# Second layer of a spectral mixture-of-experts kernel: a unit's products in two pairs of runs instead of four

## The chip, the cores and the metric

One core of a Trainium2 chip runs the whole program. The metric is device time in microseconds: the median of the runs of one kernel. Below, PE is TensorE, DVE is VectorE, ACT is ScalarE, POOL is GpSimd and SP is the engine that issues most transfers.

## The reference

Three stages follow each other, all in float32. The change touches the last alone.

```python
def _moe2_ref(x, w_in, w_out):
    h = np.maximum(x @ w_in, 0.0)          # x: 24576 x 256, w_in: 256 x 2048
    return (h * h @ w_out)                 # w_out: 2048 x 256

def reference(**kwargs):
    attn_out = _attn_ref(...)              # filter by FFT over 3072 positions, 8 x 3072 x 256
    x = attn_out.reshape(B * S, D)
    x = _moe_ref(x=x, ...)                 # each token through one of 8 experts (256 -> 1024 -> 256)
    return _moe2_ref(x=x, ...)             # every token through a dense layer with squared ReLU
```

## The kernel before

The filter, the routing and the first (expert) layer come first; the second layer runs when they are done, from about 1775 us to the end. A float32 operand is held as two parts, a high part and the rest (`bh` and `bl` for x, `wsh` and `wsl` for w_in, `hh` and `hl` for the squared hidden values, `woh` and `wol` for w_out), and a product is made of three matmuls: high x high, high x rest, rest x high. Every matmul of this layer has a 128x128 stationary operand, which a weight load brings (LDWEIGHTS, PEld in the rows), and 256 moving columns.

The layer works on 48 tiles of 512 tokens (`NTILE2`), each in 8 units of 256 hidden values (`NU`): 384 units. A unit has two halves.

`up2` forms x @ w_in for a unit. By a scheme of Strassen's kind (seven block products in place of eight) it makes products with indices 0 to 6, three matmuls each, 21 in all. Three PSUM banks take them: V (`psH`, two buffers, tile name `ph`), G (`psX`, one buffer, tile name `px`) and P (`psH2`, one buffer, tile name `ph` too). V and G are added onto in stages: V holds product 0, then 0+4, then 0+4+5, then all with 2, and between two stages a copy or an addition reads it: ACT's copies `s1` (after 0), `u2` (after 4) and the last into `C[:, 2]`; DVE's addition into `C[:, 3]` (after 5). G holds product 3, which ACT copies to `p5`, then 3+6, which DVE adds into `C[:, 1]`. P holds product 1, which DVE adds into `C[:, 0]`. The next stage of a bank may start only when the reader of the stage before has ended. Below, V0, G3, P1, V4, G6, V5, V2 are the bank and the index of a product (a bank's name and a first index), and C0, C1, C3 the three additions. At the end DVE makes `q`, the squared ReLU of all four blocks of C.

`split_h` splits `q` for the second matrix: `hh` is a copy to the high part on ACT, `hl` the rest on DVE (q minus hh). `down2` multiplies them with w_out, 24 matmuls, and adds onto the tile's two banks `py` over its 8 units; at a tile's last unit ACT copies these (`ou`) and POOL sends the rows out.

All three are generators, and the loop in `steps_m` fixes by hand the order in which they issue: in turn n it advances `up2` of unit n, `split_h` of unit n-1 and `down2` of unit n-2. Each engine runs its instructions in that order. So TensorE's row in a turn is V0 G3, 3 of `down2`, P1 V4, 6, G6 V5, 9, V2, 6: four pairs of an `up2` run and a `down2` run. Once in a tile `split_t` prepares the next tile's operand in four steps at the ends of four turns: copies on ACT and subtractions on DVE (`tc` among them).

Of the kernel before, what the change touches and what calls it, by code (L numbers as in the profile page):

```python
# [17 lines left out]
ALU = mybir.AluOpType  # L18
# [84 lines left out]
def spectral_moe_kernel(ctx: ExitStack, tc: tile.TileContext, x, filt_r, filt_i, w_gate, w_og, w1, w2,  # L103
                        w_in, w_out, c_ma, c_mi, c_mb, c_mb2, c_sg, c_cum, out):
    nc = tc.nc
# [608 lines left out]
    def py_tiles(t):  # L714
        return [pl["psY2" if t % 2 and "psY2" in pl else "psY"].tile([128, TT], F32, name=f"py{h}") for h in range(2)]
# [82 lines left out]
    def up(t, f):  # L798
        xh, xl = X[t]
        w = width[t]  # L800
        h1, l1 = (a[:, 0] for a in W[t, f // 2])
        f2 = f % 2
        ps = ph_tile()[:, 0:w]
        n = 0
        for c in range(2):
            for a, b in ((h1, xh), (h1, xl), (l1, xh)):
                nc.tensor.matmul(ps, a[:, c, f2 * 128:(f2 + 1) * 128], b[:, c, 0:w], start=n == 0, stop=n == 5)  # L807
                n += 1
        hh = pl["hp"].tile([128, TT], F32R, name="hh")[:, 0:w]
        hl = pl["hp"].tile([128, TT], F32R, name="hl")[:, 0:w]  # L810
        nc.scalar.activation(hh, ps, AF.Relu)  # L811
        tick[:] = [hh[0:1, 0:1].bitcast(F32)]
        nc.vector.scalar_tensor_tensor(hl, ps, 0.0, hh.bitcast(F32), op0=ALU.max, op1=ALU.subtract)  # L813
        H[t, f] = hh, hl
# [77 lines left out]
    def up2(t, u):  # L892

        bh, bl, _ = X2[t]
        wsh, wsl = w2nd[0:2]

        def prod(ps, a, b, start):
            for n, (x, y) in enumerate(((wsh, bh), (wsh, bl), (wsl, bh))):
                nc.tensor.matmul(ps, x[:, u, a], y[:, b], start=start and n == 0, stop=n == 2, skip_group_check=True)  # L899

        bank = lambda name: pl[name].tile([128, TT], F32, name="px" if name == "psX" else "ph")[:, 0:256]
        V, G, P = bank("psH"), bank("psX"), bank("psH2")
        s1, p5, u2 = (pl["sp"].tile([128, 256], F32, name=n) for n in ("s1", "p5", "u2"))
        C = pl["cp"].tile([128, 4, 256], F32, name="C")
        prod(V, 0, 0, True)
        nc.scalar.copy(s1, V)
        prod(G, 3, 3, True)
        nc.scalar.copy(p5, G)
        yield
        prod(P, 1, 1, True)  # L910
        nc.vector.tensor_tensor(C[:, 0], P, s1, ALU.add)
        prod(V, 4, 4, False)
        nc.scalar.copy(u2, V)  # L913
        yield
        prod(G, 6, 2, False)
        prod(V, 5, 5, False)
        nc.vector.tensor_tensor(C[:, 3], V, p5, ALU.add)  # L917
        nc.vector.tensor_tensor(C[:, 1], G, u2, ALU.add)
        yield
        prod(V, 2, 6, False)  # L920
        nc.scalar.copy(C[:, 2], V)  # L921
        q = pl["cp"].tile([128, 4, 256], F32, name="q")
        nc.vector.scalar_tensor_tensor(q, C, 0.0, C, op0=ALU.max, op1=ALU.mult)  # L923
        H2[t, u] = q
        yield

    def split_h(t, u):
        q = H2[t, u]
        hh, hl = (pl["h2p"].tile([128, 4, 256], F32R, name=n) for n in ("hh2", "hl2"))
        nc.scalar.copy(hh, q)  # L930
        yield
        nc.vector.tensor_tensor(hl, q, hh.bitcast(F32), ALU.subtract)  # L932
        H2[t, u] = hh, hl
        yield

    def down2(t, u):

        hh, hl = H2[t, u]
        woh, wol = w2nd[2:4]
        if u == 0:  # L940
            Z[t] = [p.rearrange("p (c d) -> p c d", c=2) for p in py_tiles(t)]
        for m in range(24):
            k, i, c, n = m // 12, m // 6 % 2, m // 3 % 2, m % 3
            x, w = ((hh, woh), (hl, woh), (hh, wol))[n]
            nc.tensor.matmul(Z[t][k][:, c, :], x[:, 2 * i + k, c * 128:(c + 1) * 128], w[:, 2 * u + i, :],  # L945
                             start=u == 0 and m in (0, 12), stop=u == NU - 1 and m in (11, 23), skip_group_check=True)
            if u == NU - 1 and m in (11, 23):
                if k == 0:
                    Z[t].append(pl["oup"].tile([128, 4, D], F32, name="ou"))
                ou = Z[t][2]  # L950
                nc.scalar.copy(ou[:, 2 * k:2 * k + 2, :], Z[t][k])  # L951
                io = X2[t][2]
                for c in range(2 * k, 2 * k + 2):
                    nc.gpsimd.indirect_dma_start(out=outv[4 * t + c], out_offset=bass.IndirectOffsetOnAxis(ap=io[:, c:c + 1], axis=0),  # L954
                                                 in_=ou[:, c, :], in_offset=None)
            if m in (2, 8, 17):
                yield
        del H2[t, u]
        if u == NU - 1:
            del X2[t], Z[t]  # L960
        yield
# [3 lines left out]
    units2 = [(t, u) for t in range(NTILE2) for u in range(NU)]  # L965
# [3 lines left out]
    def step_1(t, f):  # L969

        last = t + 1 == KP
        if f == 5 and t + 2 == KP:
            start_t(KP)
        if f == 1 and t + 1 >= KP:
            for n in (t + 2, t + 3) if last else (t + 3,):
                if n < NMAIN:
                    start_t(n)
        if f == 1 and last:
            gather(KP)
        if f == 3 and t + 2 < NMAIN and t + 2 != KP:  # L980
            gather(t + 2)
        if f % 2 == 1:

            g = NQ * t + f // 2 + 2
            if NQ * KP <= g < NQ * NMAIN:
                split_w(*divmod(g, NQ))
            if NQ * KP <= g + 2 < NQ * NMAIN:
                load_w(*divmod(g + 2, NQ))
        if t + 1 < NMAIN:
            at = (4, 5, 7) if last else (2, 4, 6)  # L990
            if f == at[0]:
                scale_x(t + 1)
            if f == at[0] + 1:
                put_ids(t + 1)
            if f in at[1:]:
                turn_x(t + 1, at.index(f) - 1)
        elif f == 1:
            load_t(0)
            load_t(1)
        if f not in (1, 5) and dec and next(dec[0], 0) == 0:  # L1000
            dec.clear()
            dcs.close()
            pl["bp0"] = ctx.enter_context(tc.tile_pool(name="bp0", bufs=1))
            pl["bp0"].tile([128, 16], F32, name="pad0")
        if t + 1 == NMAIN and f >= 3:
            if f == 3:
                first.append(split_t(0))
            next(first[0], None)

    def extra(t):  # L1010

        start_t(t)
        gather(t)
        for q in range(3):
            load_w(t, q)
        scale_x(t)
        put_ids(t)
        turn_x(t, 0)
        turn_x(t, 1)
        for f in range(NF + 1):  # L1020
            if f < NF:
                if f % 2 == 0:
                    split_w(t, f // 2)
                    if f == 0:
                        load_w(t, 3)
                up(t, f)
            if f:
                down(t, f - 1)

    def steps_m():  # L1030
        for n in range(len(jobs) + LAG1):
            if n < len(jobs):
                t, f = jobs[n]
                up(t, f)
                step_1(t, f)
            if n >= LAG1:
                down(*jobs[n - LAG1])
            yield
        used = nc.values_load(usedi[0:1, 0:1], min_val=0, max_val=NTILE_T)
        with tc.If(used > NTILE_T - NX):  # L1040
            for t in range(NMAIN, NTILE1):
                extra(t)
        m1.close()
        xgs.close()
        open_m2()
        st = iter(())
        for n in range(len(units2) + 2):
            g = up2(*units2[n]) if n < len(units2) else iter(())
            t, u = units2[min(n, len(units2) - 1)]
            d = down2(*units2[n - 2]) if n >= 2 else iter(())  # L1050
            for part in range(4):
                next(g, None)
                if part == 0 and 0 < n <= len(units2):
                    sh = split_h(*units2[n - 1])
                if part in (1, 2) and n:
                    next(sh, None)
                next(d, None)
            if u == 2 and t + 2 < NTILE2:
                load_t(t + 2)
            if u == 3 and t + 1 < NTILE2:  # L1060
                st = split_t(t + 1)
            next(st, None)
            yield
# [41 lines left out]
    gens = {"a": steps_a(), "b": steps_b(), "c": steps_c()}  # L1105
    done = {"a": 0, "b": 0, "c": 0}
    m = steps_m()
    dec = []
    pre = None
    ready_m = False  # L1110
    close_at = len(order) - 1 - order[::-1].index("b") + 2
    for i, k in enumerate(order):
# [3 lines left out]
        n = done["a"]  # L1116
# [62 lines left out]
```

## Time and profile before

| | |
|---|---|
| median of 3 runs | 3820.49 us (3819.74 to 3821.23) |
| profiled execution | 3807.87 us, its span 3806.2 us |
| PE busy | 3757.5 us, 99% of the span |
| PE weight loads | 3510.1 us, 92% |
| DVE, ACT, POOL busy | 73%, 52%, 16% |
| granted TensorE clock, mean | 0.998 |
| chain that ended last, by line | `down2` 27%, `up2` 18% (bank `ph`) and 7% (`px`) |

The profiled execution is 12.6 us shorter than the median of the runs. A matmul's record is longer (0.28 us) than the distance between the starts of two of them (0.11 to 0.12), since they overlap and their ends are modelled; distances between starts are what counts on TensorE. The rows themselves stand further below.

### The profile page before, as it was taken

What the parts mean: (1) busy time and instruction counts of PE and PEld (TensorE: products, weight loads), DVE (VectorE), ACT (ScalarE), POOL (GpSimd) and SP (SyncE); (2) the same over time, 40 slices, a digit from 0 to 9 for tenths busy, and PEclk for the clock granted to TensorE, in tenths of its full rate; (3) what the DMA queues carried; (4) which work ended last, traced back from release to release, by engine and by line L of the source; (5) the groups of instructions that cost most, each with busy time, mean ns of one, the idle gap of its engine ahead of it and who ended that gap; (6) DMA issues with size and microseconds to landing.
All of it is one profiled execution on the core that took longest, in us unless ns stands there. A gap on an engine that the chain in (4) does not pass through costs nothing.

```text
span 3806.2 us, 73317 instructions
## 1 busy us (share of the span) xinstructions
PE 3757.5 (99%) x27256; PEld 3510.1 (92%) x27256; DVE 2769.3 (73%) x5041; ACT 1980.2 (52%) x3912; POOL 608.2 (16%) x641
## 2 busy tenths in 40 slices
PE   8999999999999999999999999999999999999998
PEld 7888877888888888888999999999999999999998
DVE  6687685688888865665777777777777777777775
ACT  6476473454554554554555555555555555555554
POOL 3477575000000000000011001000100110011001
PEclk9999999999999999999999999999999999999999
DMA  6333322455555554553000100010000001000100
GB/s 192 100 114 117 107 90 100 153 168 160 172 174 165 173 165 151 162 157 93 23 26 26 29 23 29 23 29 23 29 25 27 24 29 29 24 26 26 29 18 18
DMA packets 262750, 309.29 MB, mean 81 GB/s; under 512 B 75154, under 2 KB 206195, under 8 KB 262387
## 3 DMA queue, kind: packets, MB, share of 16 engines
q1 hardware_dynamic: 242928, 252.39, 21.9%
q0 software_dynamic: 18432, 51.93, 3.8%
q8 instruction: 215, 3.52, 0.4%
q14 instruction: 149, 1.21, 0.1%
q10 hardware_dynamic: 1026, 0.23, 0.0%
HBM read 224.01 MB, written 80.45 MB: 80 GB/s over the span
## 4 chain that ended last, share of the span: by engine, by line
PE 52%; issue 1%; POOL 0%; POOLq 0%; DVE 0%; ACT 0%; DVEq 0%; ACTq 0%
PE py L945 27%; PE ph L899 18%; PE px L899 7%; POOL out_dram L954 0%; POOLq L1174 0%; DVE C L917 0%; ACT u L913 0%; DVEq L917 0%; POOLq L954 0%; ACTq L913 0%
## 5 line engine op out<-in xcount | busy, mean ns | idle before, releaser
L945 PE MATMUL py<-woh,hh 128*128 128x256 f32 x3072 | 857.1, 279 | 0.0
L945 PE MATMUL py<-woh,hl 128*128 128x256 f32 x3072 | 852.8, 278 | 0.5 <-DVE hl L932 0.5
L945 PE MATMUL py<-wol,hh 128*128 128x256 f32 x3072 | 852.9, 278 | 0.0
L954 POOL DMA_INDIRECT out_dram<-ou,ix x192 | 214.0, 1115 | 2924.3 <-ACT ou L951 2880.5
L945 PEld LDWEIGHTS py<-woh,hl 128*128 128x128 f32 x3072 | 579.9, 189 | 1.0 <-DVE hl L932 0.9
L945 PEld LDWEIGHTS py<-woh,hh 128*128 128x128 f32 x3072 | 579.9, 189 | 0.0
L945 PEld LDWEIGHTS py<-wol,hh 128*128 128x128 f32 x3072 | 576.3, 188 | 0.0
L811 ACT ACTIVATE hh<-ph 128x512 fp32r<-128x512 f32 (+1 forms) x472 | 252.2, 534 | 577.4 <-PE ph L807 560.6
L899 PE MATMUL ph<-bh,wsh 128*128 128x256 f32 x1920 | 540.8, 282 | 6.0 <-SPq L1040 4.8
L899 PE MATMUL ph<-bl,wsh 128*128 128x256 f32 x1920 | 537.1, 280 | 0.0
L899 PE MATMUL ph<-bh,wsl 128*128 128x256 f32 x1920 | 536.8, 280 | 0.0
L813 DVE SCALAR_TENSOR_TENSOR hl<-ph,hh 128x512 fp32r<-128x512 f32 (+1 forms) x472 | 286.5, 607 | 254.8 <-ACT hh L811 254.1
L923 DVE SCALAR_TENSOR_TENSOR q<-C 128x1024 f32<-128x1024 f32 x384 | 470.5, 1225 | 1.8 <-ACT C L921 1.8
L932 DVE TENSOR_TENSOR hl<-q,hh 128x1024 fp32r<-128x1024 f32 x384 | 466.8, 1216 | 1.1 <-ACT hh L930 1.1
L917 DVE TENSOR_TENSOR C<-ph,p 128x256 f32<-128x256 f32 x384 | 163.3, 425 | 412.7 <-ACT hh L930 403.1
L921 ACT COPY C<-ph 128x256 f32<-128x256 f32 x384 | 144.1, 375 | 525.2 <-PE ph L899 525.2
L930 ACT CAST hh<-q 128x1024 fp32r<-128x1024 f32 x384 | 403.5, 1051 | 1.3 <-DVE q L923 1.3
L899 PEld LDWEIGHTS ph<-bh,wsh 128*128 128x128 f32 x1920 | 362.4, 189 | 7.2 <-issue 4.9
L899 PEld LDWEIGHTS ph<-bh,wsl 128*128 128x128 f32 x1920 | 360.9, 188 | 0.0
L899 PEld LDWEIGHTS ph<-bl,wsh 128*128 128x128 f32 x1920 | 360.9, 188 | 0.0
L824 PE MATMUL py<-hh,wh 128*128 128x512 f32 (+1 forms) x944 | 341.0, 368 | 0.0
L807 PE MATMUL ph<-xh,wh 128*128 128x512 f32 (+1 forms) x944 | 339.3, 359 | 0.0
(265 smaller groups left out, 8086.7 us busy)
## 6 DMA issues: line engine op xcount, KB each, us to landing
r<-in_moe_w_dram SPq DMA_DIRECT2D x448, 256.0 KB
xt<-in_x_dram SPq DMA_DIRECT2D x48, 512.0 KB
r<-ytd SPq DMA_DIRECT2D x48, 512.0 KB
xg<-srt SPq DMA_DIRECT2D x41, 544.0 KB
ytd<-yt SPq DMA_DIRECT2D x41, 512.0 KB
xg<-srt SPq DMA_DIRECT2D x18, 272.0 KB
ytd<-yt SPq DMA_DIRECT2D x18, 256.0 KB
raw<-in_moe_w_in_dram SPq DMA_DIRECT2D x16, 256.0 KB
```

Of the source, the lines that this page charges most:

```text
L807: nc.tensor.matmul(ps, a[:, c, f2 * 128:(f2 + 1) * 128], b[:, c, 0:w], start=n == 0, stop=n == 5)
L811: nc.scalar.activation(hh, ps, AF.Relu)
L813: nc.vector.scalar_tensor_tensor(hl, ps, 0.0, hh.bitcast(F32), op0=ALU.max, op1=ALU.subtract)
L824: nc.tensor.matmul(Y[t][h], a[:, f % 2, h * 128:(h + 1) * 128], b, start=f == 0 and i == 0, stop=f == NF - 1 and i == 2, skip_group_check= ...
L899: nc.tensor.matmul(ps, x[:, u, a], y[:, b], start=start and n == 0, stop=n == 2, skip_group_check=True)
L917: nc.vector.tensor_tensor(C[:, 3], V, p5, ALU.add)
L921: nc.scalar.copy(C[:, 2], V)
L923: nc.vector.scalar_tensor_tensor(q, C, 0.0, C, op0=ALU.max, op1=ALU.mult)
L930: nc.scalar.copy(hh, q)
L932: nc.vector.tensor_tensor(hl, q, hh.bitcast(F32), ALU.subtract)
L945: nc.tensor.matmul(Z[t][k][:, c, :], x[:, 2 * i + k, c * 128:(c + 1) * 128], w[:, 2 * u + i, :], start=u == 0 and m in (0, 12), stop=u == ...
L954: nc.gpsimd.indirect_dma_start(out=outv[4 * t + c], out_offset=bass.IndirectOffsetOnAxis(ap=io[:, c:c + 1], axis=0), in_=ou[:, c, :], in_o ...
```

## The change

`up2` gets another place to stop: after V0, then after G3, then after P1, V4 and G6, then after V5; V2 comes last. `down2` stops after 6 and after 15 matmuls and at its end, no longer after 3, 9 and 18. The loop advances them in another order: V0 of unit n, V2 of unit n-1 (kept as `old`), G3, P1 V4 G6 (18 matmuls of `up2`), then 15 of `down2`, V5 (3), and the other 9 of `down2`. `hh` of unit n-1 is issued ahead of the 15, `hl` behind them. The addition C1 moves from behind C3 to directly behind G6.

```diff
--- before.py
+++ after.py
@@ -904,6 +904,7 @@
         C = pl["cp"].tile([128, 4, 256], F32, name="C")
         prod(V, 0, 0, True)
         nc.scalar.copy(s1, V)
+        yield
         prod(G, 3, 3, True)
         nc.scalar.copy(p5, G)
         yield
@@ -911,11 +912,11 @@
         nc.vector.tensor_tensor(C[:, 0], P, s1, ALU.add)
         prod(V, 4, 4, False)
         nc.scalar.copy(u2, V)
-        yield
         prod(G, 6, 2, False)
+        nc.vector.tensor_tensor(C[:, 1], G, u2, ALU.add)
+        yield
         prod(V, 5, 5, False)
         nc.vector.tensor_tensor(C[:, 3], V, p5, ALU.add)
-        nc.vector.tensor_tensor(C[:, 1], G, u2, ALU.add)
         yield
         prod(V, 2, 6, False)
         nc.scalar.copy(C[:, 2], V)
@@ -953,7 +954,7 @@
                 for c in range(2 * k, 2 * k + 2):
                     nc.gpsimd.indirect_dma_start(out=outv[4 * t + c], out_offset=bass.IndirectOffsetOnAxis(ap=io[:, c:c + 1], axis=0),
                                                  in_=ou[:, c, :], in_offset=None)
-            if m in (2, 8, 17):
+            if m in (5, 14):
                 yield
         del H2[t, u]
         if u == NU - 1:
@@ -1044,17 +1045,24 @@
         xgs.close()
         open_m2()
         st = iter(())
+        none = iter(())
+        old = none
         for n in range(len(units2) + 2):
-            g = up2(*units2[n]) if n < len(units2) else iter(())
+            g = up2(*units2[n]) if n < len(units2) else none
             t, u = units2[min(n, len(units2) - 1)]
-            d = down2(*units2[n - 2]) if n >= 2 else iter(())
-            for part in range(4):
-                next(g, None)
-                if part == 0 and 0 < n <= len(units2):
-                    sh = split_h(*units2[n - 1])
-                if part in (1, 2) and n:
-                    next(sh, None)
-                next(d, None)
+            d = down2(*units2[n - 2]) if n >= 2 else none
+            next(g, None)
+            next(old, None)
+            sh = split_h(*units2[n - 1]) if 0 < n <= len(units2) else none
+            next(g, None)
+            next(g, None)
+            next(sh, None)
+            next(d, None)
+            next(d, None)
+            next(sh, None)
+            next(g, None)
+            next(d, None)
+            old = g
             if u == 2 and t + 2 < NTILE2:
                 load_t(t + 2)
             if u == 3 and t + 1 < NTILE2:
```

In a steady unit TensorE's row around V4 and G6 read before (`ph` from V4, then six of `down2`, then `px` of G6; G3's last matmul stands seven rows further up):

```order
L899 MATMUL ph<-bh,wsh 128x256 [waits Activation_49]
L899 MATMUL ph<-bl,wsh 128x256
L899 MATMUL ph<-bh,wsl 128x256
L945 MATMUL py_22212<-woh,hh_22367 128x256
L945 MATMUL py_22212<-woh,hl_22368 128x256
L945 MATMUL py_22212<-wol,hh_22367 128x256
L945 MATMUL py_22212<-woh,hh_22367 128x256
L945 MATMUL py_22212<-woh,hl_22368 128x256
L945 MATMUL py_22212<-wol,hh_22367 128x256
L899 MATMUL px<-bh,wsh 128x256 [waits Activation_49]
L899 MATMUL px<-bl,wsh 128x256
L899 MATMUL px<-bh,wsl 128x256
```

and reads now (from G3's last matmul over P1 and V4 to G6):

```order
L899 MATMUL px<-bh,wsl 128x256
L899 MATMUL ph<-bh,wsh 128x256
L899 MATMUL ph<-bl,wsh 128x256
L899 MATMUL ph<-bh,wsl 128x256
L899 MATMUL ph<-bh,wsh 128x256 [waits Activation_49]
L899 MATMUL ph<-bl,wsh 128x256
L899 MATMUL ph<-bh,wsl 128x256
L899 MATMUL px<-bh,wsh 128x256 [waits Activation_49]
L899 MATMUL px<-bl,wsh 128x256
L899 MATMUL px<-bh,wsl 128x256
L946 MATMUL py_22227<-woh,hh_22368 128x256
```

Between G3 and G6 there now stand the six matmuls of P1 and V4.

ScalarE's row for one unit, before (`s`, `p`, `u` are the copies s1, p5, u2; the row with C is the copy after V2; L930 is `hh` of the unit ahead):

```order
L906 COPY s_22480<-ph 128x256 [waits PE_49,Activation_49]
L908 COPY p_22481<-px 128x256 [waits PE_49,Activation_49]
L913 COPY u_22482<-ph 128x256 [waits PE_49,Activation_49]
L930 CAST hh_22503<-q 128x1024 [waits DVE_49]
L921 COPY C<-ph 128x256 [waits PE_49,Activation_49]
```

and now (L922 is the copy after V2 of the unit ahead):

```order
L906 COPY s_22474<-ph 128x256 [waits PE_49,Activation_49]
L922 COPY C<-ph 128x256 [waits PE_49,Activation_49]
L909 COPY p_22475<-px 128x256 [waits PE_49,Activation_49]
L914 COPY u_22476<-ph 128x256 [waits PE_49,Activation_49]
L931 CAST hh_22504<-q 128x1024 [waits DVE_49]
```

The copy into C moved from the end of the unit to behind s1 of the next, ahead of `p5` and `hh`.

VectorE's row, before (L911, L917, L918 are C0, C3, C1; L932 is `hl` of the unit ahead, L923 is `q`):

```order
L911 TENSOR_TENSOR C<-ph,s_22546 128x256 [waits PE_49,Activation_49]
L917 TENSOR_TENSOR C<-ph,p_22547 128x256 [waits PE_49,Activation_49]
L918 TENSOR_TENSOR C<-px,u_22548 128x256 [waits Activation_49]
L932 TENSOR_TENSOR hl_22570<-q,hh_22569 128x1024 [waits Activation_49]
L923 SCALAR_TENSOR_TENSOR q<-C 128x1024 [waits DVE_49,Activation_49]
```

and now (L924 is `q` of the unit ahead, L912, L916, L919 are C0, C1, C3, L933 is `hl` of the unit ahead):

```order
L924 SCALAR_TENSOR_TENSOR q<-C 128x1024 [waits DVE_49,Activation_49]
L912 TENSOR_TENSOR C<-ph,s_22540 128x256 [waits PE_49]
L916 TENSOR_TENSOR C<-px,u_22542 128x256 [waits PE_49,Activation_49]
L933 TENSOR_TENSOR hl_22571<-q,hh_22570 128x1024 [waits Activation_49]
L919 TENSOR_TENSOR C<-ph,p_22541 128x256 [waits PE_49]
```

C3 moved behind `hl`, and `hl` now belongs to the same unit as the `q` at the top of the row.

## Rows read from the trace of the kernel before

**Rows 1.** Busy time by stretch, TensorE, second layer: us, busy (matmuls), granted clock, DMA

```profile
1900.00:2000.00 100.00, 100.00 (x860) 1.00 0.09 27
```

**Rows 2.** Chain of waits over one unit: start us, us, what, count

```profile
3002.19 0.35 PE ph L899 x3
...
3003.26 0.69 PE ph L899 x6
3003.95 0.68 PE py L945 x6
3004.63 0.35 PE px L899 x3
...
3005.34 1.06 PE py L945 x9
3006.40 0.35 PE ph L899 x3
...
3007.44 0.12 PE ph L899
```

**Rows 3.** Chain of waits, the same over a unit near 3240 us

```profile
3240.17 0.71 PE py L945 x6
...
3241.58 1.02 PE py L945 x9
```

**Rows 4.** Instructions on tile q, 1900 to 3200 us: count: ns min/median/max, first to last

```profile
L923 DVE SCALAR_TENSOR_TENSOR q<-C x248: 1217/1226/1229, 1900.1 to 3196.1; 128x1024 f32<-128x1024 f32 x124
```

**Rows 5.** The same view of tile q, 3223.5 to 3297 us

```profile
L932 DVE TENSOR_TENSOR hl<-q,hh x14: 1214/1216/1216, 3226.7 to 3294.7; 128x1024 fp32r<-128x1024 f32 x14
```

**Rows 6.** Instructions in time, TensorE near 3221 us: start, us, engine, line, operation

```profile
3221.39 0.39 PE L899 MATMUL ph<-bh,wsh 128*128 128x256 f32 x1
```

**Rows 7.** Instructions in time, TensorE near the tail

```profile
3789.17 0.38 PE L945 MATMUL py<-woh,hl 128*128 128x256 f32 x1
3789.39 0.28 PE L945 MATMUL py<-wol,hh 128*128 128x256 f32 x1
...
3789.73 0.28 PE L945 MATMUL py<-wol,hh 128*128 128x256 f32 x1
```

**Rows 8.** Instructions in time, head of the layer, V0 to V4 (PEld: weight loads)

```profile
1780.77 0.28 PE L899 MATMUL ph<-bh,wsl 128*128 128x256 f32 x1
...
1781.08 0.38 ACT L906 COPY s<-ph 128x256 f32<-128x256 f32 x1
...
1781.51 0.19 PEld L899 LDWEIGHTS ph<-bh,wsh 128*128 128x128 f32 x1
1781.56 0.33 PE L899 MATMUL ph<-bh,wsh 128*128 128x256 f32 x1
...
1781.73 0.28 PE L899 MATMUL ph<-bl,wsh 128*128 128x256 f32 x1
...
1781.85 0.28 PE L899 MATMUL ph<-bh,wsl 128*128 128x256 f32 x1
```

**Rows 9.** Instructions in time, a steady unit: TensorE, ScalarE and DVE

```profile
3001.23 0.28 PE L899 MATMUL ph<-bh,wsl 128*128 128x256 f32 x1
...
3001.60 0.38 ACT L921 COPY C<-ph 128x256 f32<-128x256 f32 x1 [0.53 <-PE ph L899]
...
3002.01 1.23 DVE L923 SCALAR_TENSOR_TENSOR q<-C 128x1024 f32<-128x1024 f32 x1
...
3005.79 0.41 DVE L918 TENSOR_TENSOR C<-px,u 128x256 f32<-128x256 f32 x1
...
3006.12 1.22 DVE L932 TENSOR_TENSOR hl<-q,hh 128x1024 fp32r<-128x1024 f32 x1
```

**Rows 10.** Groups by line, 1800 to 3780 us: busy us, mean ns, idle before

```profile
L930 ACT CAST hh<-q 128x1024 fp32r<-128x1024 f32 x377 | 396.2, 1051 | 0.0
```

**Rows 11.** Instructions in time, head of the layer, C3 and the next weight load

```profile
1783.32 0.42 DVE L917 TENSOR_TENSOR C<-ph,p 128x256 f32<-128x256 f32 x1 [0.63 <-PE ph L899]
...
1783.80 0.19 PEld L899 LDWEIGHTS ph<-bh,wsh 128*128 128x128 f32 x1 [0.80 <-DVE C L917]
```

More of the change, by code (lines that the diff above doesn't have):

```diff
@@ L913, in up2 @@
         nc.scalar.copy(u2, V)
+        prod(G, 6, 2, False)
+        nc.vector.tensor_tensor(C[:, 1], G, u2, ALU.add)
         yield
-        prod(G, 6, 2, False)
         prod(V, 5, 5, False)
         nc.vector.tensor_tensor(C[:, 3], V, p5, ALU.add)
-        nc.vector.tensor_tensor(C[:, 1], G, u2, ALU.add)
         yield
```

## The prediction

> **What bounds the kernel now.** The change touches only the second layer: 384 units of 45 matmuls (21 of `up2`, 24 of `down2`), more than half of the span. The table of stretches comes first [rows 1]: between 1900 and 2000 us TensorE is busy all the time, at a granted clock of 1.00, the upper of its two levels (2.4 GHz). So TensorE's own queue sets the time there, and another engine matters only where it makes TensorE wait. Next comes the chain of waits over one unit [rows 2]: only runs of matmuls, nothing else ends last. A unit starts at 3002.19 and the next at 3007.44, 5.25 us; over a long stretch the squared ReLU `q` comes 248 times between 1900.1 and 3196.1 us [rows 4], so 1296.0 / 247 = 5.247 us.
>
> The reader is to see in rows 2 that matmuls of one shape run at two paces. Six of `down2` take 0.68 us, 0.1133 each (call it fast); nine others take 1.06, 0.1178 each (slow). The pace stays through an `up2` run and the `down2` run behind it and changes where the next `up2` run starts: a unit's four pairs of runs (9, 12, 15 and 9 matmuls) last 1.07, 1.37, 1.77 and 1.04 us, that is slow, fast, slow, fast. With 24 slow and 21 fast the two paces give 2.827 + 2.379 = 5.206; the other 0.04 is the way between paces, some 0.011 for a pair.
>
> The pace is no matter of which products run. Near 3221 us a matmul was held up [rows 6], and from there the same program runs the other way round: around 3240 us the 9 `down2` matmuls that were slow take 1.02 and 6 that were fast take 0.71 [rows 3]. There are then 21 slow matmuls in a unit, and `hl` comes every (3294.7 - 3226.7) / 13 = 5.231 us [rows 5]. So it alternates from pair to pair, and a wait can turn it over.
>
> **The change part by part.** Nothing is added or removed: the same matmuls, copies and vector operations, the same number of each, no other transfer. Three things move.
>
> *1. Four pairs become two.* A unit now has a pair of 33 and a pair of 12. If the pace still alternates from pair to pair, the 33 always have one pace and the 12 the other. Long pair fast: 33 x 0.1133 + 12 x 0.1178 + 2 x 0.011 = 5.175 us, 0.072 less than now. Long pair slow: 33 x 0.1178 + 12 x 0.1133 + 0.022 = 5.27, 0.023 more. Over some 382 full units that is -27 or +9 us, if nothing waits.
>
> *2. The sixth product (G again, tile `px`) comes closer to the copy that it needs.* It adds onto the bank that the fourth product (G3) filled, and ScalarE must have copied that bank to `p5` first. Before, 15 matmuls stood between (3 of `down2`, P and V4, 6 of `down2`); now only P and V4, 6. How long the copy's way is, the head of the layer shows, where there are no `down2` products and V4 stands just so behind V0 [rows 8]: the last matmul of V0 starts at 1780.77, ScalarE's copy at 1781.08 (0.31 later, 0.38 long), and the waiting weight load at 1781.51, 0.05 behind the copy's end. Six fast intervals, 0.68, were over at 1781.45: 0.06 late, and the product's second matmul indeed stands 0.17 behind the first (1781.56, 1781.73) instead of 0.11. In steady units the copy starts later, 0.37 behind the last matmul (3001.23 to 3001.60) [rows 9]. So the way is 0.37 + 0.38 + 0.05 = 0.80 us, against six intervals of 0.68 (fast) or 0.71 (slow): the weight load waits 0.12 or 0.09 in every unit. Behind it in TensorE's queue stand the rest of that product and the 15 `down2` matmuls, so the whole stream moves back by it, as it did in the head; its other copies do not come closer than 9 matmuls (V0 to V4), about 1.02 to 1.06 us.
>
> Whether 0.31 or 0.37 holds is worth 0.06 x 382 = 23 us, and the order of ScalarE decides it: `p5` waits there for TensorE and for ScalarE's own earlier write, before and after alike, as the copy in rows 9 does, which starts late. So I take 0.37; by 0.31 the wait is 0.06 or 0.03. The Trainium skill's Perfetto Trace Analysis (Identifying Dependency Chains) says that an instruction waiting on several engines may get separate EventSemaphore instructions ahead of it. By that rule the later start belongs to the double wait and stays in the changed kernel; the trace agrees, with 0.37 in a steady unit.
>
> *3. V2 moves behind the next unit's V0, and with it everything on DVE.* DVE's order was C0, C3, C1, `hl`, `q`; it becomes `q` (of the unit ahead), C0, C1, `hl`, C3. That closes a ring: V2, copy to C2, `q`, `hh`, `hl`, C3, and C3 must have read V's bank before the next V2. From the last matmul of V2: 0.37 to the copy, 0.41 to `q` (3001.60 to 3002.01), `q` 1.23 [rows 9], up to 0.08 to `hh` (an estimate from the other hand-offs, 0.03 to 0.06), `hh` 1.05 [rows 10], 0.04, `hl` 1.22 less 0.08 of overlap (the DVE operation ahead of `hl` ends at 3006.20, `hl` starts at 3006.12), C3 0.42, and 0.06 to the weight load (1783.32 + 0.42 to 1783.80) [rows 11]: 4.80 us. The load is due three intervals less than a period later: 5.29 - 0.34 = 4.95 at the shortest of the two sums below. It has at least 0.15 us to spare, so this hides. Once in a tile the four `tc` subtractions of the next tile, of C3's shape (0.42 each), stand between C3 and `q`, 1.7 us where DVE has about 1.4 free: up to 0.3 late, half of it covered, 0 to 7 us over 47 tiles. I take 1, because operations of this size overlap by 0.08 each in rows 9.
>
> *Ends of the layer.* In the head the waits get shorter (products of the next unit now stand between), at the tail the last V2 has fewer matmuls behind it. Both are single waits of under 1 us; taken together as 0, with 1 us either way.
>
> *Sum.* With the wait of 2, long pair fast: 5.175 + 0.12 = 5.295, +0.048 a unit, +18 us. Long pair slow: 5.27 + 0.09 = 5.36, +0.113, +43 us. Which it is, the rows leave open: after the wait of 0.06 in the head the next interval is slow (1781.73 to 1781.85) [rows 8], at 3221 us a wait kept the slow pace where it should have ended [rows 6], while near the tail a matmul 0.22 behind its predecessor left the fast pace as it was (3789.39 to 3789.73, three intervals) [rows 7], and that delay, 0.11, is the nearest in size. So I take the middle, +30, and 1 for the tiles. The profiled execution took 3807.87 us; by the sum it becomes 3839. The runs' median, 3820.49, is 12.6 us above that execution, and the same 31 on it gives 3851.
>
> On the paces themselves the Trainium skill speaks against this change: TensorE: Matmul & The Clock Gate (Wait — 56ns, not 53.3ns?) gives warm matmuls one spacing, columns / 2.4 GHz plus about 2.5 ns, 109 ns here whatever their order. The trace differs, with 113 and 118; by that rule point 1 falls away and only the wait of 2 is left, which at the mean spacing of 5.247 / 45 = 0.1166 is 0.80 - 0.70 = 0.10, or +38 us.
>
> **The rivals.**
>
> *a. No wait at G6, long pair fast: faster.* Place: the weight load of G6. It decides from the point where ScalarE's `p5` is done six intervals after G3. Price -27 us, 3793. For it: 0.072 a unit is what the paces promise where nothing waits. Against it: even the shortest way in the trace, 0.74 from 1780.77 to 1781.51, is longer than 0.68.
>
> *b. One pace for all.* The alternation is bound to the old runs. If all become fast: 45 x 0.1133 + 0.12 = 5.22, -0.027 a unit, -10 us, 3810. All slow: 45 x 0.1178 + 0.09 = 5.39, +0.144, +55, 3876. For it: a wait in every unit can set the pace anew each time. Against it: through 247 units the alternation held.
>
> *c. The ring of 3 is late.* From 0.15 us more than summed, TensorE waits at V2 in every unit as well; 0.1 us beyond that is 38 us on top, 3889. For it: six hand-offs in a row, each with its own error. Against it: every one was read.
>
> *d. A wait smaller than worked out, 0.06 to 0.03, with the paces either way:* 5.175 + 0.06 gives -5 us, 3816; 5.27 + 0.03 gives +20, 3841.
>
> **How the numbers follow.** The forecast (wait in every unit, paces alternating) 0.66, its own range 3836 to 3866; a 0.09; b 0.12, in equal parts; c 0.05; d 0.08. Faster by over 0.2% (7.6 us, about what a measurement of this kernel can tell from no change): a, half of b's fast case (0.03) and 0.04 for what I cannot name, 0.16. Within 0.2%: the other half of that case, d with the long pair fast (0.04), and 0.03 of the rest, 0.10. Slower: 0.74. The range leaves out a, and the upper ends of c: 3806 to 3878.
>
> **What would show it.** On PE's line, a matmul of `px` with a record longer than 0.28 us and its weight load waiting for ACT's `p` copy, once a unit, 0.09 to 0.12 late; the next matmul 0.2 or more behind. In the chain of waits, ACT's `p` between runs of PE. Two paces, 33 of one and 12 of the other; a period of `q` of 5.29 to 5.36 us. On DVE, C3 directly behind `hl`, and V2's weight load not waiting for it. The forecast is wrong if G6's load starts with no delay, if V2's waits in every unit, or if the period is under 5.247.

## The result, and the profile after

The changed kernel takes 3860.56 us (median of 4 runs, 3859.31 to 3861.83) where the kernel before took 3820.86 on the same chip (4 runs, 3819.74 to 3822.87): a ratio of 1.0105, 95% interval 1.009 to 1.012, 39.7 us slower. The forecast was 31 us slower.

The profiled execution took 3859.31 us, 51 more than the profiled one of before. Not all of that is the change: this execution began the second layer 14.0 us later (first matmul of the layer at 1789.53 instead of 1775.50 us), in code that the change leaves alone. That goes with the chip and not with the order: one kernel of the experiments, run on two chips, begins the layer at 1774.21 and at 1788.54. From the layer's first matmul to its last it is 1789.53 to 3846.78 = 2057.25 us, against 1775.50 to 3795.36 = 2019.86: 37.4 us more. That is what has to be explained.

The table of stretches for TensorE, as [rows 1] (us, busy and count, granted clock, DMA):

```profile
1900.00:2000.00 100.00, 100.00 (x846) 1.00 0.10 28
```

TensorE is busy all the time as before, at the same clock, and does 14 matmuls less. So a share of busy time says nothing here of what was lost. The period says it, by tile `q` as in [rows 4]:

```profile
L924 DVE SCALAR_TENSOR_TENSOR q<-C x244: 1224/1226/1228, 1903.1 to 3199.9; 128x1024 f32<-128x1024 f32 x122
```

1296.8 / 243 = 5.337 us a unit, 0.090 more than the 5.247 of before; over 382 units 34 us.

The chain of waits over a unit and a half, as [rows 2] (start us, us, what, count):

```profile
3001.39 0.78 PE ph L899 x6
3002.17 0.34 PE px L899 x3
3002.52 0.68 PE ph L899 x6
3003.20 0.46 PE px L899 x3
3003.65 1.76 PE py L946 x15
...
3005.77 1.02 PE py L946 x9
...
3007.85 0.71 PE ph L899 x6
3008.56 0.44 PE px L899 x3
3009.00 1.76 PE py L946 x15
```

Still nothing but runs of matmuls; ScalarE's `p`, which the prediction expected between them as a sign, does not appear. The reader is to see the second `px` run of each unit, which is G6: three matmuls in 0.46 and 0.44 us where three at the fast pace take 0.34 and three at the slow pace 0.35. That is 0.12 more after a fast `ph` run (six in 0.68, P1 and V4), and 0.09 more after a slow one (0.71). The instructions in time show where it comes from (start us, us, engine, line, operation):

```profile
3002.24 0.28 PE L899 MATMUL px<-bh,wsl 128*128 128x256 f32 x1
...
3002.61 0.37 ACT L909 COPY p<-px 128x256 f32<-128x256 f32 x1
...
3002.92 0.28 PE L899 MATMUL ph<-bh,wsl 128*128 128x256 f32 x1
3003.03 0.19 PEld L899 LDWEIGHTS px<-bh,wsh 128*128 128x128 f32 x1
3003.03 0.38 PE L899 MATMUL px<-bh,wsh 128*128 128x256 f32 x1
...
3003.26 0.28 PE L899 MATMUL px<-bl,wsh 128*128 128x256 f32 x1
```

G3's last matmul starts at 3002.24; ScalarE's copy into `p5` 0.37 later, as in a steady unit of before [rows 9], not 0.31 as in the head [rows 8]; it lasts 0.37; G6's weight load starts 0.05 behind its end, together with its matmul, where other loads run one interval ahead. The way is 0.79 us, and the next matmul stands 0.23 behind. How often that happens is in the records of the one matmul that waits, grouped by line and form (count, busy us, mean ns, idle us before). Before:

```profile
L899 PE MATMUL px<-bh,wsh 128*128 128x256 f32 x768 | 216.6, 282 | 0.0
```

and after:

```profile
L899 PE MATMUL px<-bh,wsh 128*128 128x256 f32 x768 | 248.8, 324 | 0.1
```

Half of these 768 are G3 and half G6. 248.8 - 216.6 = 32.2 us over 384 G6 is 0.084 us each. The distances between starts in the same trace say a little more: in the 381 turns that have all 45 matmuls, G6's second matmul stands 0.222 us behind its first where P1 and V4 had the fast pace (110 turns) and 0.198 where they had the slow pace (271), which is 0.11 and 0.08 above a plain interval, 0.088 in the mean and 33.6 us in all. The idle column stays at 0.1: a matmul that starts 0.1 us late begins before its predecessor's record ends, so its wait is counted as busy time. It shows in longer records and in the distance between starts alone.

VectorE, compared with [rows 5] and [rows 9], does what the diff says, `hl` and C3 one behind the other, with the 0.08 of overlap:

```profile
3005.01 1.23 DVE L933 TENSOR_TENSOR hl<-q,hh 128x1024 fp32r<-128x1024 f32 x1 [0.45 <-ACT hh L931]
...
3006.16 0.42 DVE L919 TENSOR_TENSOR C<-ph,p 128x256 f32<-128x256 f32 x1
```

C3 ends at 3006.58, V2's load follows at 3006.87: no wait in such a unit. In 30 of the 381 turns, never twice in a tile, there is one, by the starts 2.4 us in all. The 0.78 in the chain above is V2 in a turn in which `tc` of the next tile came first on VectorE:

```profile
3001.07 0.42 DVE L919 TENSOR_TENSOR C<-ph,p 128x256 f32<-128x256 f32 x1 [0.19 <-PE ph L899]
...
3001.55 0.19 PEld L899 LDWEIGHTS ph<-bh,wsh 128*128 128x128 f32 x1
3001.58 0.35 PE L899 MATMUL ph<-bh,wsh 128*128 128x256 f32 x1
...
3001.77 0.28 PE L899 MATMUL ph<-bl,wsh 128*128 128x256 f32 x1
```

C3 ends at 3001.49, the load starts 0.06 later, and the next matmul stands 0.19 behind.

### The profile page after: what moved, and what is told of

It is laid out like the page before. It is cut to its first block, busy times and chain, and to the rows that moved or that the text cites. A ratio compares the mean times of both kernels' runs of the same rounds, so it can differ in the third digit from the quotient of the medians.

```text
span 3857.6 us, 72840 instructions
## 1 busy us (share of the span) xinstructions
PE 3799.3 (98%) x27256; PEld 3541.4 (92%) x27256; DVE 2782.6 (72%) x5041; ACT 2026.6 (53%) x3912; POOL 608.1 (16%) x641
## 4 chain that ended last, share of the span: by engine, by line
PE 51%; issue 2%; POOL 0%; DVE 0%; ACT 0%; POOLq 0%
PE py L946 27%; PE ph L899 17%; PE px L899 8%; POOL out_dram L955 0%; DVE q L924 0%; DVE hl L933 0%; ACT hh L931 0%; POOLq L1182 0%; DVE C L919 0%; ACT C L922 0%; ACT p L909 0%; ACT ou L952 0%; ACT s L906 0%; POOLq L955 0%
## 5 line engine op out<-in xcount | busy, mean ns | idle before, releaser
L924 DVE SCALAR_TENSOR_TENSOR q<-C 128x1024 f32<-128x1024 f32 x384 | 470.7, 1226 | 371.1 <-ACT C L922 339.6
L933 DVE TENSOR_TENSOR hl<-q,hh 128x1024 fp32r<-128x1024 f32 x384 | 473.1, 1232 | 174.7 <-ACT hh L931 174.7
L906 ACT COPY s<-ph 128x256 f32<-128x256 f32 x384 | 143.6, 374 | 675.5 <-PE ph L899 675.5
L807 PE MATMUL ph<-xl,wh 128*128 128x512 f32 (+1 forms) x944 | 337.9, 358 | 0.7 <-DVE xl L792 0.7
```

## The experiments

The theory was that G6's wait for `p5` makes the loss and the paces decide how much of it is left. Its rivals were that the new order on VectorE (C3 behind `hl`) makes it, or that the paces alone do. Every kernel is compared with runs of the kernel before on its own chip in the same session; these chips differ by some 15 us (3806.1, 3818.38, 3819.98 and 3820.62 us). Below, a unit's time is worked out from first and last `q` and their count, as above.

**One edit each: G3 ahead of V2, or C3 ahead of `hl`.** The first puts nine matmuls between G3 and G6 (V2, P1, V4) in place of six; on ScalarE it puts the copy into `p5` ahead of the copy after V2:

```diff
         nc.scalar.copy(s1, V)
-        yield
         prod(G, 3, 3, True)
...
             sh = split_h(*units2[n - 1]) if 0 < n <= len(units2) else none
             next(g, None)
-            next(g, None)
```

> The changed kernel with one thing moved: G3 stands directly behind V0, ahead of the last V of the unit ahead, so that nine matmuls stand between G3 and G6. Theory (the loss is G6's wait for ACT's p5 copy, 0.09 us in each unit, and the pace alternates from pair to pair): no weight load of G6 waits any more, at least 30 us go, and a unit takes 5.175 us with the long pair fast (3793 us) or 5.27 with it slow (3829 us), the same value in nearly all units. Rival 1 (the ring over C3 and the next V2 is what is late): V2 still waits, no change, 3860 us. Rival 2 (the wait only hides a pace that belongs to the new order): the wait goes but the time moves by less than 10 us.

The second leaves TensorE's row as it is after the change and puts C3 ahead of `hl` on VectorE:

```diff
             next(d, None)
             next(d, None)
-            next(sh, None)
             next(g, None)
+            next(sh, None)
             next(d, None)
```

> The changed kernel with DVE's C3 ahead of hl instead of behind it (V5 is issued before hl), so that hl is no longer in the ring that ends at the next V2; the order on TensorE is the same. Theory (G6's wait is the loss): G6 waits as before, only the waits of V2 that come once in a tile go: 2 to 5 us, 3855 to 3859 us. Rival 1 (the ring is the loss): back to 3821 us or less.

And the two together:

> Both edits together: G3 directly behind V0, and C3 ahead of hl on DVE. Theory: no wait of TensorE in a steady unit at all; two paces alternate, so all units are alike: 5.175 us with the long pair fast (3793 us) or 5.27 with it slow (3829 us). Rival 2: near 3850 us. It is faster than the kernel before if the long pair falls on the fast pace, slower if not.

Measured: G3 first 3781.64 us, ratio 0.9934 (0.9921 to 0.9948), 24.5 us faster than before. C3 first 3840.27, 1.009 (1.0076 to 1.0104), 34.2 slower. Both 3779.66, 0.9928 (0.9915 to 0.9942), 26.4 faster. So the wait at G6 makes the loss: with it the two pairs lose in every run, without it they gain in five runs of six, whatever the order on VectorE.

The order on VectorE is worth the few us between C3 first (34.2 slower than before) and the kernel as changed (39.7 and 36.7). The first `ph` matmul of each product, after the change:

```profile
L899 PE MATMUL ph<-bh,wsh 128*128 128x256 f32 x1920 | 543.2, 283 | 6.9 <-SPq L1041 4.9 <-DVE C L919 1.9
```

and with C3 first:

```profile
L899 PE MATMUL ph<-bh,wsh 128*128 128x256 f32 x1920 | 541.6, 282 | 5.2 <-SPq L1041 4.8 <-DVE C L919 0.2
```

Idle time put down to C3 falls from 1.9 to 0.2 us and busy time by 1.6. The 1.9 are a single wait, in the layer's first turns, where V2 stands still until C3 behind `hl` has ended:

```profile
1799.44 0.38 PE L899 MATMUL ph<-bh,wsh 128*128 128x256 f32 x1 [1.94 <-DVE C L919]
```

The 1.6 go with the waits at V2 that come in 30 of the turns; with C3 first no turn has one. First to last matmul the layer takes 2052.37 us with C3 first, 4.9 less than in this trace of the changed kernel and 2.8 less than in a second one (2055.19). In both, most of the difference lies ahead of the end of the first unit's `down2` (13.64 us in place of 16.47 and 16.26).

The two faster kernels have **two times**. Five of six runs of G3 first took 3780.24 to 3782.23 us and one 3817.29; five of six of both took 3776.57 to 3780.37 and one 3814.07. The slower one, 11 and 8 us over before, is what the forecast called the long pair slow. The chain in that execution of both edits:

```profile
3001.24 1.77 PE py L945 x15
...
3003.36 1.02 PE py L945 x9
```

and the same kernel, run again on another chip, where five of five runs were of the faster kind (3789.87 to 3795.15 against 3819.98 before: 0.9927, 0.9913 to 0.994):

> The kernel with both edits once more, on whatever chip this call gets. Theory: most runs with the long pair fast, 26 us (0.7%) under the kernel before, the odd run with it slow, 9 us over; 36 us between the two.

```profile
3003.43 1.70 PE py L945 x15
...
3005.48 1.06 PE py L945 x9
```

Long pair slow and the nine fast, then the reverse. The units take 5.267 us (247 `q`, 1899.9 to 3195.5) and 5.173 (252 `q`, 1901.0 to 3199.5); the forecast had 5.27 and 5.175. 0.094 x 382 = 36 us is the distance between the two times.

**Turn the alternation over once.** In one turn, the eleventh, the 15 of `down2` are issued as 6 and 9 with P1, V4 and G6 between, so that this unit has three pairs in place of two; the rest is the kernel with both edits:

```diff
+            if n == 10:
+                next(d, None)
             next(g, None)
             next(sh, None)
-            next(d, None)
+            if n != 10:
+                next(d, None)
             next(d, None)
```

> Both edits, and in one unit of 384, the eleventh, the pairs are three instead of two (6 of down2 stand between V2 and P1). Theory (the pace is a state that turns over at each start of an up2 run and keeps what it has otherwise): from there on the other pair is the slow one, so this kernel takes the other of the two times: 36 us from the kernel with both edits, up or down. Rival (the pace belongs to a place in the program): within 2 us of it.

Nine of eleven runs took 3812.82 to 3815.73 us and two 3777.51 and 3779.14 (median 3813.26, ratio 1.0002, 0.9979 to 1.0025). The odd pair exchanges the two times. The chain around it, in a run of the slower kind:

```profile
1824.22 1.06 PE py L945 x9
...
1826.31 0.68 PE py L945 x6
1826.99 0.71 PE ph L899 x6
...
1828.06 1.06 PE py L945 x9
...
1829.47 1.02 PE py L945 x9
...
1832.62 1.77 PE py L945 x15
```

The nine at a unit's end are slow ahead of it (1.06) and fast behind (1.02), and the 15, fast in every turn before, are slow in each of the 373 full turns behind it. So the pace does alternate from pair to pair, over hundreds of units, from a start that is not always the same.

**Double the suspected wait.** The copy into `p5` is issued twice:

```diff
         nc.scalar.copy(p5, G)
+        nc.scalar.copy(p5, G)
```

> The changed kernel with ACT's p5 copy issued twice (the second copy of the same values to the same place), so that G6 has to wait for the second. Theory (the wait stands on the path in full): ACT issues copies of this size 0.27 us apart, G6's weight load waits 0.35 to 0.4 us in each unit, and the time rises by 0.27 x 382 = 103 us over the changed kernel (95 to 115). Rival (a wait of this size is partly taken up by weight loads and matmuls queued ahead): clearly less, under 60 us.

3984.55 us, beside 3855.06 for the changed kernel in the same session:

> The changed kernel once more, beside the other runs of this call: 35 to 40 us above the kernel before on this chip. Theory: about 34 us of it are G6's wait (0.09 us a unit), some 5 are waits of V2 once in a tile, and the pace gives next to nothing, since the wait sets it anew in each unit.

(that one again 36.7 us over before, 1.0097, 1.0082 to 1.0113). 129.5 us more is 0.34 a unit, more than the 95 to 115 us expected. The chain:

```profile
3000.38 0.37 ACT s L906
3000.76 0.35 ACT C L923
3001.11 0.36 ACT p L909
...
3001.50 0.38 ACT p L910
...
3001.92 0.62 PE px L899 x3
```

Now ScalarE stands in the chain by name: s1, the copy into C2 and the two into `p5`, then G6. The second copy writes what the first wrote and is not overlapped with it: it starts 0.41 after the first and 0.03 behind its end. (The first starts at 3001.09, below; the chain has 3001.11, since it counts a copy only from the end of the one ahead.) And the first starts sooner than in the changed kernel, 0.32 behind G3's last matmul in place of 0.37:

```profile
3000.77 0.28 PE L899 MATMUL px<-bh,wsl 128*128 128x256 f32 x1
...
3001.09 0.37 ACT L909 COPY p<-px 128x256 f32<-128x256 f32 x1
```

So the way is 0.35 longer, and 0.34 of it arrive in the time: whatever is added to the copy's way is paid by the whole stream; nothing behind G6 takes it up. The 0.32 also shows what the 0.37 goes with. In the changed kernel a separate semaphore instruction (ACTq, ScalarE's sequencer) waits ahead of each copy into `p5`; with two copies the second alone waits for ScalarE's own earlier write, and the first has no such instruction. The copies `s1`, `u2` and into C2 lose theirs too and start 0.32 behind as well. The instructions on the copy's line, 1900 to 3200 us, in the changed kernel:

```profile
L909 ACTq EVENT_SEMAPHORE  x244: 17/17/17, 1903.0 to 3199.8; - x122
```

and with the copy doubled, where no ACTq line is left:

```profile
L909 ACT COPY p<-px x228: 373/374/374, 1903.6 to 3194.4; 128x256 f32<-128x256 f32 x114
```

**Other pairs.** With both edits and the pairs cut at 18 up with 21 down and 3 with 3 (`down2` stops after 6 and 21), and with a single pair of 21 up and 24 down. Of the first, what it has beside both edits:

```diff
-            if m in (5, 14):
+            if m in (5, 20):
```

> Both edits (G3 directly behind V0, C3 ahead of hl), and the pairs are 18 up with 21 down and 3 up with 3 down. Theory (two paces that alternate from pair to pair, 0.1133 and 0.1178 us a matmul): with the long pair fast a unit is 39 x 0.1133 + 6 x 0.1178 + 0.022 = 5.148 us, 38 us under the kernel before; with it slow 39 x 0.1178 + 6 x 0.1133 + 0.022 = 5.296, 19 us over it; runs fall in one or the other, 57 us apart, and none between unless a wait turns the pace over on the way. Rival (a pace needs more than 3 matmuls to set in, or does not alternate any more with so short a pair): something between, -10 to 0 us.

> One pair of runs in a unit: 21 up (V5 and V2 of the unit ahead among them, at least nine matmuls between the stages of a bank), then 24 down; on DVE C3 of the unit ahead, hl, C0, q, C1. Theory (the pace turns over at each start of an up2 run): units are fast and slow by turns, 45 x 0.1133 and 45 x 0.1178 with 0.022 for two units, 5.21 us on average, 14 us under the kernel before in every run, with one time and not two, since neither start leaves more slow units than the other. Rival (the pace belongs to the pair's place in the unit): all units alike, 5.11 or 5.31 us, 52 us under or 24 over.

The first took 3835.58 us, 1.0038 (1.0024 to 1.0052), its five runs between 3826.26 and 3836.99, so none at the faster of the two times expected. Its chain begins in the fast case and is turned over by one wait (in the nine `ph`, 1.30 in place of 1.02; V2 waits for C3):

```profile
1922.62 2.38 PE py L945 x21
...
1926.40 1.30 PE ph L899 x9
...
1928.06 2.47 PE py L945 x21
...
1931.94 1.06 PE ph L899 x9
```

From there it stays slow: 5.291 us over the stretch (246 `q`, 1901.5 to 3197.9). That wait cost not its own 0.28 alone: the units behind it take 0.14 more each (5.29 in place of 5.15 from one three-matmul `down2` run to the next). Two waits in the same place before it, at 1843 and 1885 us, 0.21 and 0.23 long by the starts where this one is 0.25, had left the pace as it was.

The single pair took 3807.49 us, 0.9972 (0.9962 to 0.9981), 10.9 faster, in ten runs between 3805.85 and 3810.73, one time and not two:

```profile
2500.66 2.83 PE py L945 x24
...
2505.88 2.72 PE py L945 x24
```

One pair a unit means that whole units are slow and fast in turn (24 in 2.83 and in 2.72), so no start is better than another.

**Where the buffers lie.** The kernel keeps 64 bytes a partition (`pad2`) ahead of the second layer's buffers. With both edits and that pad left out, at 96 and at 192 bytes (the last is shown):

```diff
-        right(ctx, "pad2", 1).tile([128, 16], F32, name="pad2")
+        right(ctx, "pad2", 1).tile([128, 48], F32, name="pad2")
```

> Both edits, and the 64-byte pad ahead of the second layer's operand buffers is left out, so that all of these (x parts, hidden parts, copies) lie 64 bytes elsewhere, against the weights that keep their place. If the slow pace comes from where the two operands of a matmul lie against each other, the slow or the fast pace changes, or the pace no longer alternates (one time, or other units than 5.173 and 5.267 us). If it is a state of TensorE's own pipeline, nothing changes but perhaps which pair is the slow one.

> Both edits, and that pad is 96 bytes instead of 64, so that the operand buffers lie 32 bytes further. Same alternatives as with the pad left out.

> Both edits with a pad of 192 bytes, 128 more than the 64 of the kernel. Without the pad every matmul took 0.120 us, with 64 bytes 0.113 or 0.118 by turns, with 96 bytes a mixture. If only the place within 128 bytes counts, this is the kernel with both edits again: units of 5.173 or 5.267 us, 26 us under the kernel before or 9 over. If larger distances count, another pace: 5.40 us a unit (58 us over) or all fast, 5.11 (50 us under).

Without the pad 3878.06 us, 1.0152 (1.0136 to 1.0167), and no paces: every run, of nine or of three, has 0.120 us a matmul, and the unit takes 5.400:

```profile
2501.43 1.08 PE py L944 x9
2502.51 0.36 PE ph L898 x3
...
2503.23 1.08 PE ph L898 x9
```

With 96 bytes 3852.49 us, 1.0082 (1.0066 to 1.0097), 5.332 a unit. With 192 bytes 3817.68, 0.9992 (0.9982 to 1.0002), 5.241 a unit, and the paces turn at another place:

```profile
2499.42 1.71 PE py L945 x15
2501.13 0.34 PE ph L899 x3
2501.47 1.06 PE py L945 x9
...
2503.25 1.06 PE ph L899 x9
```

V5's three are fast with the 15 ahead of them, and the nine of `down2` behind V5 are slow: the change comes at the start of a `down2` run, not of an `up2` run. So the paces are bound to where the layer's buffers lie. The pad moves the copies' tiles along with the operands, and no run moves them apart, so that it is the operands' place is not shown. By which rule stays open too: the four pads make no simple series, and 64 and 192 bytes, 128 apart, do not behave alike.

## Why the prediction was right

- **G6's wait (step 2)** came where it was put and nearly as long as worked out: a way of 0.79 us for 0.80, 0.11 after fast and 0.08 after slow intervals for 0.12 and 0.09. The start 0.37 behind the last matmul, on which 23 us hung, stayed, for the reason given: where the copy has one wait and no separate instruction, it starts at 0.32. The Trainium skill's Perfetto Trace Analysis (Identifying Dependency Chains) says that an instruction that waits on several engines may get separate waits ahead of it; the trace agrees, with 0.37 for a copy with two waits in steady units of before and after.
- **The size of it** was less than in the sum: 32.2 us in the records of G6, 33.6 by the starts, where the middle of the two cases had 0.105 x 382 = 40. The wait behind fast matmuls is the rarer case, 110 turns of 381, and each of the two is 0.01 shorter than worked out.
- **The paces (step 1)** are the term that failed as put. "Long pair fast" or "long pair slow" holds in the kernel with both edits, to 0.003 us. In the changed kernel the wait stands inside the long pair and turns the pace there: all 110 turns that had the fast pace up to the wait have the slow pace behind it, and of the 271 with the slow pace 100 have the fast pace behind it (in the second trace 135 of 135, and 146 of 246). The chain after shows it, six `ph` in 0.68 followed, behind the wait, by 15 in 1.76. So neither case is reached: the units are a mixture, and the paces pay little. The layer's 37.4 us are 34.1 in the 381 full turns and 3.3 at its ends. Of the 34.1, G6 has 33.6 and V2 2.4, which leaves -1.9 for the paces. The middle of the cases had -27 and +9, so -9. That the paces gained 7 us less than summed and the wait cost 6 us less cancels in the total, which is luck. Rival b had this reason in it ("a wait in every unit can set the pace anew") but made one pace for all of it.
- **The ends of the layer** were put at 0 with 1 us either way and cost 3.3, some 2.2 in the first turns and 1.1 in the last: the wait of 1.94 us at V2 in the first turns is no wait "of under 1 us".
- By the Trainium skill's TensorE: Matmul & The Clock Gate (Wait — 56ns, not 53.3ns?) matmuls back to back have one spacing, and with no paces the sum was +38; the time came nearer to that than to mine, since the paces paid nearly nothing here, not since there are none. The 109 ns for 256 columns, an estimate from its formula, no run shows: the layer's matmuls, each with a weight load of its own, have 113, 118 and, without the pad, 120.
- **The ring on VectorE (step 3)** hides in ordinary units, as worked out. The tile's turn with `tc` was sized at 1 us within bounds of 0 to 7 and measured at 2.4 (3.0 in the second trace). The subtractions are not covered by their overlap: V2 waits, by 0.08 in the turn shown above (0.19 for 0.11).
- **Rival a** (no wait) is what G3 first makes, -24.5 us in most runs for the -27 worked out. **Rival c** (V2 late in every unit) and **d** (a smaller wait) did not happen.

The version that beats both kernels is the one with both edits: 26 and 28 us under before in two sessions, except for the executions that fall into the other pace (1 of 11, 8 us over before). The single pair gains 10.9 and has no such second case.

## What to carry to other kernels

When runs of one engine are made longer, count what then stands between a bank's last product and the next product onto it: here a way of 0.8 us (0.37, copy 0.37, 0.05) is longer than six matmuls of 256 columns, which cost 0.08 us or more in every one of 384 units; with nine no wait was left. An engine that is 100% busy can still be waiting; read the distance between starts, and the run lengths in the chain, not idle time. And put a moved copy's user as far behind as the order allows before looking at anything else: three more matmuls in between took the change from 37 to 40 us slower to 25 faster in five runs of six. Look also for a copy that waits for its own engine's earlier write beside the producer: here that costs 0.05 us of the way.

## What the runs showed of the hardware

- Matmuls of one shape at one granted clock (0.996 to 0.998 in all runs, the upper level) run at 0.1133 or 0.1178 us each by turns, or all at 0.120 (with 96 bytes a mixture from 0.113 to 0.125), by where in SBUF the layer's buffers lie: 64 bytes of padding are worth 5.400 less 5.173 us in a unit of 45, 4%.
- The pace is a state: its alternation lasts hundreds of units, it turns at switches between two operand sets (at which of them differs with the pad) and can be turned by a wait of 0.08 to 0.25 us, not by every one. One program so has two times, 36 us (1%) apart, that no view of busy time tells apart.
- A copy on ScalarE that writes the tile of the copy ahead of it starts 0.03 us behind that one's end and 0.41 behind its start (copies of 0.37 us at 3001.09 and 3001.50); two copies into different tiles stood 0.35 apart here, the second 0.02 ahead of the first one's end (3002.26 + 0.37 = 3002.63, and 3002.61).
- A copy on ScalarE that waits for TensorE and for ScalarE's own earlier write starts 0.37 us behind the last matmul, one that waits for TensorE alone 0.32 (0.31 in the head of the layer); a semaphore instruction of its own stands ahead of the first kind alone.
